# Float64 words to float32 in five steps with an integer add, and raw quarters of w_out loaded into the place of W

## The chip, the cores and the metric

The kernel runs on one core of a Trainium2 chip. The metric is the device time of one execution in microseconds (us). Its engines are TensorE (PE in the profile, with PEld for its weight loads), VectorE (DVE), ScalarE (ACT), GpSimd (POOL) and SyncE (SP), which here only issues transfers.

## The reference

Three parts follow each other, in float32, save that two of the weights reach the chip as raw float64:

```python
k_p = k.reshape(B, H, Sp, 8, D).mean(axis=3)          # keys and values pooled by 8
attn = softmax(q @ k_p.T / sqrt(D)); x = attn @ v_p    # 8 heads, 4608 tokens, 512 wide
logits = x @ phi                                       # 8 experts x 4 slots
slot_input = softmax(logits, axis=0).T @ x
slot_out[e] = maximum(slot_input[e] @ w1[e], 0) @ w2[e]
x = softmax(logits, axis=1) @ slot_out
h = x @ w_in                                           # w_in, w_out: float64 on arrival
solu = h * softmax(h)
ln = (solu - mean) / sqrt(var + 1e-6) * g_ln
out = ln @ w_out
```

## The kernel before

There are three stages. In the attention stage the tokens go in 12 blocks of 384; a scheduler of the language orders the instructions of PE, DVE, ACT and POOL there, from a list of due times. In the experts' stage 32 slot rows pass through eight experts: `first(e)` (L674) multiplies by w1, `second(e, fh)` (L835) by w2, half an expert at a time, for `x` from 0 to 15. Between the halves other work is written out by hand or fitted in by the scheduler: the combine weights are copied (`combine_copies`, L792, tile c), turned (L799, pc) and split (L801 on ACT, L802 on DVE, tile cS), and the two float64 weights are converted. In the last stage, from the first h (L949) on, 36 tiles of 128 tokens go through the h product, the softmax, the layer norm and the product with w_out (L1108 to L1111), in an order written by hand.

w_in and w_out arrive in four raw quarters each, 128 x 2048 words of 4 bytes (1 MB): o0 to o3 for w_out, i0 to i3 for w_in. The two words of a float64 lie side by side. A conversion makes a float32: ACT takes the absolute value of the high word, scaled (L715), DVE shifts it by three bits (L735), puts the sign in (L736), makes a power of two of the exponent (L737), multiplies it with the low word (L745), and POOL adds the two in float (L731). The quarters of w_in go to four tiles win0 to win3, which the product pM (L889) reads after the last `second`. Those of w_out go to yo; ACT squares them for a sum over all (L755, into W_lo as scratch), and `out_scale` (L760 to L766: the product pq, a power on POOL, the scales gs) waits for all four. Then come W_hi (L769, eight on ACT) and W_lo (L772, eight on DVE): here called the W stage, at x == 9.

SP issues transfers in the order written: `SEQ` names them, o and i for raw quarters, b for the w2 of an expert (two of 1 MB), a for w1, W for the tiles win (no transfer). Raw quarters take one of two buffers of `rawp`, w1, w2 and win a ring of 88 KB a partition. A transfer whose buffer isn't free waits at the head of SP's queue, and all behind it wait too. `CI` says ahead of which x a quarter is converted, `DUM` after which x a product without use is put that keeps PE busy (L861, spare).

Of the kernel before, what the change touches and what calls it, by code (L numbers as in the profile page):

```python
# [19 lines left out]
P = 128  # L20
# [8 lines left out]
DM = 512  # L29
# [16 lines left out]
PST = 0  # L46
LP = ()
LS = 2
OL = 0
# [3 lines left out]
for e_, m_ in AP: BESIDE[e_] += m_  # L53
WQ = 2
WQ2 = 4
SEQ = 'o0 a1 a2 r4 b0 b1 a5 a6 o1 i0 b3 i1 b2 o2 b5 W0 o3 b6 i2 b4 i3 b7'.split()
WL = 0
NPRE = 8
OA = ((1,), (1,), (1,), (1,), (1,), (1,), (1,), (1,), (1,), (1,), (1,), (1,))
# [24 lines left out]
def moe_attention_kernel(ctx: ExitStack, tc, q, k, v, phi, w1, w2, w_in, w_out, g, out):  # L84
    nc = tc.nc
    pe, dve, act, pool, sp = nc.tensor, nc.vector, nc.scalar, nc.gpsimd, nc.sync
# [9 lines left out]
    g_sb = cpool.tile([P, NFC], F32, name="g_sb")  # L96
# [66 lines left out]
    w1t, wo_raw, w2t, wi_raw, win = {}, {}, {}, {}, {}  # L163
# [7 lines left out]
                store[e, (i + j) // 4, (i + j) % 4] = t[:, j, :]  # L171

    def load_raw(store, src, i, name):
        store[i] = (ring if OL and i == 1 and store is wo_raw else rawp).tile([P, 2048], I32, name="raw")
        sp.dma_start(store[i], src[i].bitcast(I32))

    placed = {}
# [43 lines left out]
    if True:  # L221
# [476 lines left out]
    if True:  # L698
        ex = ctx.enter_context(tc.tile_pool(name="ex", bufs=1, side="left", reuse_waits="tile"))
        cvp = ctx.enter_context(tc.tile_pool(name="cvp", bufs=2, side="left", reuse_waits="tile"))  # L700
# [3 lines left out]
        pool.memset(hTm, 0.0)  # L704


        mag, last_s = {}, [None]

        def words(raw):
            w = raw.rearrange("p (n two) -> p n two", two=2)  # L710
            return w[:, :, 0], w[:, :, 1]

        def double_size(key, raw, pl=None):
            y = mag[key] = cvp.tile([P, 1024], F32, name="cv_y") if pl is None else pl.bitcast(F32)
            act.activation(y, words(raw)[1].bitcast(F32), AF.Abs, scale=2.0 ** -112)  # L715

        def double_steps(key, dst, raw, pl=None):
            lo, hi = words(raw)
            yf = mag[key]
            y = yf.bitcast(I32)  # L720
            s = cvp.tile([P, 1024], I32, name="cv_s") if pl is None else pl.bitcast(I32)
            sf = last_s[0] = s.bitcast(F32)

            def low():

                act.activation(lo.bitcast(F32), lo.bitcast(U32), AF.Copy, scale=2.0 ** -52)

            last = (
                (lambda: pool.scalar_tensor_tensor(sf, lo.bitcast(U32), 2.0 ** -52, sf, ALU.mult, ALU.mult)) if PST else
                (lambda: pool.tensor_tensor(sf, lo.bitcast(F32), sf, ALU.mult)),  # L730
                lambda: pool.tensor_tensor(dst, yf, sf, ALU.add),  # L731
            )

            return low, (
                lambda: dve.tensor_scalar(y, y, 3, None, ALU.logical_shift_left),  # L735
                lambda: dve.scalar_tensor_tensor(y, hi, -(1 << 31), y, ALU.bitwise_and, ALU.bitwise_or),  # L736
                lambda: dve.tensor_scalar(s, y, -(1 << 23), None, ALU.bitwise_and),  # L737
            ), last

        def from_double(key, dst, raw):  # L740
            low, steps, last = double_steps(key, dst, raw)
            for f in steps:
                f()
            if True:
                dve.scalar_tensor_tensor(last_s[0], words(raw)[0].bitcast(U32), 2.0 ** -52, last_s[0], ALU.mult, ALU.mult)  # L745
            last[1]()


        yo = ex.tile([P, NFC, DM], F32, name="yo")

        def out_words(i):
            y = yo[:, 2 * i:2 * i + 2, :].rearrange("p c d -> p (c d)")
            from_double(("o", i), y, wo_raw[i])
            for c in (2 * i, 2 * i + 1):
                act.activation(W_lo[:, c, :].bitcast(mybir.dt.bfloat16), yo[:, c, :], AF.Square, scale=g_sb[:, c:c + 1], accum_out=wsq[:, c:c + 1])  # L755

        def out_scale():

            pq = psE.tile([P, NFC], F32, name="pq", tag="spare")
            pe.matmul(pq, ones, wsq, start=True, stop=True)  # L760
            dve.tensor_reduce(ws[:, 0:1], pq, axis=AX.X, op=ALU.add)
            dve.tensor_scalar(ws[:, 0:1], ws[:, 0:1], 1e-30, 2.0 ** -30, ALU.max, ALU.mult)
            pool.tensor_tensor(ws[:, 1:2], ws[:, 0:1], exps_[:, 0:1], ALU.pow)
            dve.tensor_scalar(ws[:, 1:2].bitcast(I32), ws[:, 1:2].bitcast(I32), 0x7F800000, None, ALU.bitwise_and)
            dve.reciprocal(ws[:, 2:3], ws[:, 1:2])
            dve.tensor_scalar(gs, g_sb, ws[:, 1:2], None, ALU.mult)  # L766

        def high_part(c):
# [26 lines left out]
        def combine_split(i):  # L795
            c4 = c4s.pop(i)
            pc = psE.tile([P, 4, P], F32, name="pc", bufs=2)
            for t in range(4):
                pe.transpose(pc[:, t, :], c4[:, t].rearrange("p a s -> p (a s)"), ident)  # L799
            cd = cS[:, 4 * i:4 * i + 4, :]  # L800
            act.activation(cd, pc, AF.Copy)  # L801
            dve.scalar_tensor_tensor(cd, cd.bitcast(F32), lo_rows, pc, ALU.mult, ALU.add)  # L802

        for x in SEQ[NPRE:]:
            load_next(x)

        double_size(("o", 0), wo_raw[0])
        double_size(("o", 1), wo_raw[1])
        out_words(0)
        out_words(1)  # L810
        combine_exps()
# [26 lines left out]
        for i in range(2):  # L838
            combine_copies(i)
        CE = (0, 0, 0, 2, 9, 13, 14, 14, 15)  # L840
        CI = {0: (("i", 0),), 2: (("i", 1),), 4: (("o", 2),), 6: (("o", 3),), 8: (("i", 2),), 10: (("i", 3),)}
        for x in range(2 * NE):
            for kind, i in CI.get(x, ()):
                double_size((kind, i), (wi_raw if kind == "i" else wo_raw)[i])
                if kind == "i":
                    from_double(("i", i), win[i], wi_raw[i])
                else:
                    out_words(i)
            if x == 9:
                out_scale()  # L850
                for c in range(NFC):
                    high_part(c)
                    low_part(c)
            for i in range(9):
                if CE[i] == x:
                    combine_split(i)
                    if i + 2 < 9:
                        combine_copies(i + 2)
            second(x // 2, x % 2)
            for nn in DUM.get(x, ()):  # L860
                pe.matmul(spare[:, 0:nn], ident, w2t[x // 2, x % 2, 3][:, 0:nn], start=True, stop=True)  # L861
# [38 lines left out]
        for hf in range(2):  # L900
# [327 lines left out]
```

## Time and profile before

| | |
|---|---|
| time, median of 3 runs | 461.35 us (459.4 to 462.12) |
| time of the profiled execution | 462.56 us |
| span from its first to its last instruction | 460.7 us |
[...]
| PE, DVE, ACT, POOL busy | 408.5, 340.7, 287.8, 225.3 us |
| transfers | 97.06 MB |

The 1.86 us between span and time lie outside the instructions. Times in the profile count from the span's start. The shares of busy time are averages over stages with different limits, so the experts' stage is read from timelines of its own.

### The profile page before, as it was taken

The numbers are of one execution on the slowest core, as the hardware profiler recorded it, in microseconds if no ns is written. First come the engines' busy times: TensorE is split into PE (matmuls) and PEld (weight loads), VectorE is DVE, ScalarE is ACT, GpSimd is POOL, SyncE is SP. The second block draws the span as 40 slices with busy tenths as digits, with TensorE's granted clock in tenths as the row PEclk, the third lists the DMA queues.
The fourth block names the chain that finished last, engine by engine and source line by source line (L and its number), as shares of the span: only waits on it lengthen the run. The fifth ranks groups of instructions, "written<-read, shape, count | busy, mean of one in ns | idle before, by whom it ended". The sixth has DMA issues, their size and how long they took to land. (4 is left out here: it accounts for less than half of the span.)

```text
span 460.7 us, 8267 instructions
## 1 busy us (share of the span) xinstructions
PE 408.5 (89%) x2979; PEld 229.6 (50%) x2979; DVE 340.7 (74%) x563; ACT 287.8 (62%) x645; POOL 225.3 (49%) x392
## 2 busy tenths in 40 slices
PE   4688998998999797833967999999999999999997
PEld 4376576786777424222313544444444444444445
DVE  4798498999893557785929988777878888778710
ACT  4476675995785406333624995777877886878721
POOL 4485176665341017693221566665555555565510
PEclk9778999999999787965979999999999999999999
DMA  8999986692598788999200034858659666675851
GB/s 287 421 416 419 418 324 268 195 336 101 199 370 276 234 317 368 345 379 366 95 1 0 0 94 91 167 102 188 156 104 177 160 161 114 159 159 94 161 149 56
DMA packets 84008, 97.06 MB, mean 211 GB/s; under 512 B 70017, under 2 KB 70785, under 8 KB 78849
## 3 DMA queue, kind: packets, MB, share of 16 engines
q1 hardware_dynamic: 83968, 96.55, 66.6%
q8 instruction: 23, 0.38, 0.3%
q14 instruction: 17, 0.13, 0.1%
HBM read 70.32 MB, written 9.44 MB: 173 GB/s over the span
## 5 line engine op out<-in xcount | busy, mean ns | idle before, releaser
L1108 PE MATMUL o<-W_hi,vhi 128*128 128x512 f16 x280 | 106.4, 380 | 0.7 <-ACT vhi L1017 0.6
L1109 PE MATMUL o<-W_lo,vhi 128*128 128x512 f16 x280 | 106.1, 379 | 0.0
L339 PE MATMUL sc<-BD,qT 128*128 128x144 f32 (+1 forms) x320 | 59.9, 334 | 12.0 <-ACT BD L282 7.9
L1111 PE MATMUL o<-W_hi,vlo 128*128 128x512 f16 x280 | 67.3, 379 | 0.6 <-DVE vlo L997 0.6
L377 POOL TENSOR_TENSOR a<-a,rs 128x864 f32<-128x864 f32 x23 | 37.5, 1641 | 57.0 <-DVE rs L375 45.3
L339 PEld LDWEIGHTS sc<-BD,qT 128*128 128x128 f32 (+1 forms) x320 | 45.0, 203 | 23.3 <-issue 7.8
L1088 ACT ACTIVATE v<-u,b,sr 128x1024 f32<-128x1024 f32 x33 | 40.9, 1240 | 15.1 <-POOL b L1087 15.0
L1098 DVE TENSOR_TENSOR v<-v,v 128x1024 f16<-128x1024 f32 x32 | 39.2, 1224 | 10.8 <-ACT v L1088 10.8
L1108 PEld LDWEIGHTS <-vhi 128*128 128x128 f16 x280 | 27.3, 98 | 38.6 <-issue 7.5
L1065 ACT ACTIVATE e<-u,nmu 128x1024 f32<-128x1024 f32 x33 | 37.9, 1148 | 13.5 <-POOL nmu L1064 12.8
L1060 ACT ACTIVATE e<-h,nm 128x1024 f32<-128x1024 f32 x33 | 36.7, 1111 | 13.4 <-DVE nm L1057 13.2
L1111 PEld LDWEIGHTS <-vlo 128*128 128x128 f16 x280 | 27.2, 98 | 33.5 <-DVE vlo L997 1.0
L1057 DVE TENSOR_REDUCE nm<-h 128x1 f32<-128x1024 f32 x33 | 40.1, 1220 | 3.8 <-PE h L1054 3.7
L1062 DVE CUSTOM_DVE_ANT_0 u<-h,e 128x1024 f32<-128x1024 f32 x33 | 40.3, 1221 | 3.4 <-ACT e L1060 3.0
L1109 PEld LDWEIGHTS <-vhi 128*128 128x128 f16 x280 | 27.4, 98 | 30.1 <-issue 0.9
L1097 DVE TENSOR_SCALAR v<-u,nmu,sr 128x1024 f16<-128x1024 f32 x32 | 26.0, 812 | 18.7 <-POOL sr L1074 18.6
L349 DVE TENSOR_REDUCE nmax<-sc 128x6 f32<-128x432 f32 x48 | 28.5, 600 | 10.8 <-PE sc L339 10.5
L384 PE MATMUL pt<-ident,a 128*128 128x128 f32 (+1 forms) x180 | 31.8, 285 | 1.3 <-ACT aT L391 0.8
L391 ACT ACTIVATE aT<-pt 128x384 f32<-128x384 f32 (+1 forms) x60 | 27.7, 486 | 7.2 <-PE pt L384 6.7
L1077 POOL TENSOR_SCALAR r<-sr,ws 128x1 f32<-128x1 f32 x33 | 29.1, 881 | 3.4
L1074 POOL TENSOR_TENSOR sr<-z,exponents 128x3 f32<-128x3 f32 x33 | 28.9, 877 | 2.7
L1124 ACT ACTIVATE ob<-o,r 128x512 f32<-128x512 f32 x32 | 21.4, 669 | 9.6 <-PE o L1111 9.6
(224 smaller groups left out, 773.4 us busy)
## 6 DMA issues: line engine op xcount, KB each, us to landing
w<-in_w_dram SPq DMA_DIRECT2D x16, 1024.0 KB, 9.6
vT<-in_v_dram SPq DMA_DIRECT2D x8, 1152.0 KB, 12.7
qT<-in_q_dram SPq DMA_DIRECT2D x11, 768.0 KB, 17.6
out_dram<-ob SPq DMA_DIRECT2D x11, 768.0 KB, 3.7
w<-in_w_dram SPq DMA_DIRECT2D x16, 512.0 KB, 6.9
kT<-in_k_dram SPq DMA_DIRECT2D x7, 1152.0 KB, 18.7
raw<-in_w_out_dram SPq DMA_DIRECT2D x4, 1024.0 KB, 14.1
raw<-in_w_in_dram SPq DMA_DIRECT2D x4, 1024.0 KB, 8.1
```

Of the source, the lines that this page charges most:

```text
L339: pe.matmul(sc[t0:t1, r].rearrange("p h j -> p (h j)"), qT[n][:, hp, r, t0:t1], BD[b % NBD][:, hp, :], start=True, stop=True)
L377: eng.tensor_tensor(av, av, rs.unsqueeze(3).to_broadcast([P, NR, 4, J]), ALU.mult)
L384: pe.transpose(pt[:m, r, :], a_buf[n % NA][:, r, P * c:P * c + m], ident)
L1057: dve.tensor_reduce(nm, hv, axis=AX.X, op=ALU.max, negate=True)
L1060: act.activation(e, hv, AF.Exp, bias=nm, accum_out=st[:, 0:1])
L1062: dve.tensor_tensor_reduce(u, hv, e, 1.0, 0.0, ALU.mult, ALU.add, st[:, 1:2])
L1065: act.activation(e, u, AF.Square, bias=nmu, accum_out=st[:, 2:3])
L1088: act.activation(v, u, AF.Identity, bias=b, scale=sr[:, 0:1])
L1098: eng[H2].tensor_tensor(v2, v, v1, ALU.subtract)
L1108: pe.matmul(po, hi[:, c, :], W_hi[:, c, :], start=(c == 0), stop=False)
L1109: pe.matmul(po, hi[:, c, :], W_lo[:, c, :], start=False, stop=False)
L1111: pe.matmul(po, lo[:, c, :], W_hi[:, c, :], start=False, stop=(c == NFC - 1))
```

## The change

The conversion has five steps: ACT takes the high word as before (L720 of the new kernel) and turns the low word, in place, into an integer scaled by 2 to the -29 (L721); DVE shifts and puts the sign in (L722, L723); POOL adds the two as 32-bit integers (L724). The steps L737 and L745 on DVE are gone. o2 and o3 are loaded into the memory of W_hi and W_lo instead of the buffers of `rawp`, the squares go to a scratch tile of their own (cv_q), and the W stage stands ahead of x == 4 instead of 9. `SEQ` and `CI` have a new order.

```diff
-SEQ = 'o0 a1 a2 r4 b0 b1 a5 a6 o1 i0 b3 i1 b2 o2 b5 W0 o3 b6 i2 b4 i3 b7'.split()
+SEQ = 'o0 a1 a2 r4 b0 b1 a5 a6 o1 b2 o2 o3 b3 i0 W0 b4 i1 b5 i2 b6 i3 b7'.split()
     def load_raw(store, src, i, name):
-        store[i] = (ring if OL and i == 1 and store is wo_raw else rawp).tile([P, 2048], I32, name="raw")
+        if store is wo_raw and i > 1:
+            store[i] = (W_hi, W_lo)[i - 2].rearrange("p c d -> p (c d)").bitcast(I32)
+        else:
+            store[i] = rawp.tile([P, 2048], I32, name="raw")
         sp.dma_start(store[i], src[i].bitcast(I32))
-        def double_size(key, raw, pl=None):
-            y = mag[key] = cvp.tile([P, 1024], F32, name="cv_y") if pl is None else pl.bitcast(F32)
-            act.activation(y, words(raw)[1].bitcast(F32), AF.Abs, scale=2.0 ** -112)
...
-                lambda: pool.tensor_tensor(dst, yf, sf, ALU.add),
...
-                lambda: dve.tensor_scalar(y, y, 3, None, ALU.logical_shift_left),
-                lambda: dve.scalar_tensor_tensor(y, hi, -(1 << 31), y, ALU.bitwise_and, ALU.bitwise_or),
-                lambda: dve.tensor_scalar(s, y, -(1 << 23), None, ALU.bitwise_and),
...
-                dve.scalar_tensor_tensor(last_s[0], words(raw)[0].bitcast(U32), 2.0 ** -52, last_s[0], ALU.mult, ALU.mult)
+        def from_double(dst, raw, add):
             lo, hi = words(raw)
+            y = cvp.tile([P, 1024], F32, name="cv_y")
+            yi = y.bitcast(I32)
+            act.activation(y, hi.bitcast(F32), AF.Abs, scale=2.0 ** -112)
+            act.activation(lo, lo.bitcast(U32), AF.Copy, scale=2.0 ** -29)
+            dve.tensor_scalar(yi, yi, 3, None, ALU.logical_shift_left)
+            dve.scalar_tensor_tensor(yi, hi, -(1 << 31), yi, ALU.bitwise_and, ALU.bitwise_or)
+            add.tensor_tensor(dst.bitcast(I32), yi, lo, ALU.add)
...
-        CI = {0: (("i", 0),), 2: (("i", 1),), 4: (("o", 2),), 6: (("o", 3),), 8: (("i", 2),), 10: (("i", 3),)}
+        CI = {3: (("o", 2),), 4: (("o", 3),), 7: (("i", 0),), 9: (("i", 1),), 11: (("i", 2),), 13: (("i", 3),)}
...
-            if x == 9:
+            if x == 4:
                 out_scale()
                 for c in range(NFC):
                     high_part(c)
```

On SP, in the experts' stage, the queue behind the last of expert 6's w1 stood so before (raw is a quarter, from in_w_in or in_w_out; w2_70 and w2_74 are the halves of b7):

```order
L175 DMA raw_2302<-in_w_out_dram 128x2048
L169 DMA w2_50_2304<-in_w2_dram 128x2048
L169 DMA w2_54_2306<-in_w2_dram 128x2048
L175 DMA raw_2312<-in_w_out_dram 128x2048
L169 DMA w2_60_2314<-in_w2_dram 128x2048
L169 DMA w2_64_2316<-in_w2_dram 128x2048
L175 DMA raw_2318<-in_w_in_dram 128x2048
L169 DMA w2_40_2320<-in_w2_dram 128x2048
L169 DMA w2_44_2322<-in_w2_dram 128x2048
L175 DMA raw_2324<-in_w_in_dram 128x2048
L169 DMA w2_70_2326<-in_w2_dram 128x2048
L169 DMA w2_74_2328<-in_w2_dram 128x2048
```

And so it stands in the changed kernel, its last twelve, behind b2, o2, o3 (into W_hi and W_lo) and b3:

```order
L179 DMA raw_2300<-in_w_in_dram 128x2048
L169 DMA w2_40_2306<-in_w2_dram 128x2048
L169 DMA w2_44_2308<-in_w2_dram 128x2048
L179 DMA raw_2310<-in_w_in_dram 128x2048
L169 DMA w2_50_2312<-in_w2_dram 128x2048
L169 DMA w2_54_2314<-in_w2_dram 128x2048
L179 DMA raw_2316<-in_w_in_dram 128x2048
L169 DMA w2_60_2318<-in_w2_dram 128x2048
L169 DMA w2_64_2320<-in_w2_dram 128x2048
L179 DMA raw_2322<-in_w_in_dram 128x2048
L169 DMA w2_70_2324<-in_w2_dram 128x2048
L169 DMA w2_74_2326<-in_w2_dram 128x2048
```

All of w_out now comes ahead of w_in; i0 to i3 (raw_2300 to raw_2322) share the two buffers of `rawp` with o0 and o1 alone, and i3 with b7 behind it is last as before.

On POOL, the adds of the conversions stand among the copies c of the combine weights. Before, from the copy behind the add of i0 on:

```order
L792 TENSOR_TENSOR c_2415<-L_all,cr 128x512
L731 TENSOR_TENSOR win_2309<-cv_y,cv_s 128x1024
L792 TENSOR_TENSOR c_2424<-L_all,cr 128x512
L792 TENSOR_TENSOR c_2449<-L_all,cr 128x512
L792 TENSOR_TENSOR c_2538<-L_all,cr 128x512
L731 TENSOR_TENSOR yo<-cv_y,cv_s 128x1024
L792 TENSOR_TENSOR c_2573<-L_all,cr 128x512
L792 TENSOR_TENSOR c_2588<-L_all,cr 128x512
L731 TENSOR_TENSOR yo<-cv_y,cv_s 128x1024
L763 TENSOR_TENSOR ws<-ws,exponents 128x1
L731 TENSOR_TENSOR win_2310<-cv_y,cv_s 128x1024
L731 TENSOR_TENSOR win_2311<-cv_y,cv_s 128x1024
```

Now, from the second copy behind the add of o2 on (W_lo holds the raw words of o3):

```order
L771 TENSOR_TENSOR c_2405<-L_all,cr 128x512
L724 TENSOR_TENSOR yo<-cv_y,W_lo 128x1024
L771 TENSOR_TENSOR c_2414<-L_all,cr 128x512
L771 TENSOR_TENSOR c_2431<-L_all,cr 128x512
L771 TENSOR_TENSOR c_2524<-L_all,cr 128x512
L742 TENSOR_TENSOR ws<-ws,exponents 128x1
L771 TENSOR_TENSOR c_2563<-L_all,cr 128x512
L724 TENSOR_TENSOR win_2302<-cv_y,raw 128x1024
L771 TENSOR_TENSOR c_2578<-L_all,cr 128x512
L724 TENSOR_TENSOR win_2303<-cv_y,raw 128x1024
L724 TENSOR_TENSOR win_2304<-cv_y,raw 128x1024
L724 TENSOR_TENSOR win_2305<-cv_y,raw 128x1024
```

The adds of w_out and the power ws moved ahead of all four adds of w_in.

On ACT, the low words of o0 and o1 are converted in the attention stage, in its fifth block of 12. Before, from the end of the fourth block's transposes on:

```order
L281 ACTIVATE BD_206<-kp 64x2x72
L282 ACTIVATE BD_206<-kp 64x2x72
L315 ACTIVATE WT<-pw_809 32x144 x4
L355 ACTIVATE a_225,ssum<-sc_761,nmax 128x72 x6
L361 ACTIVATE a_225<-dd_207 128x3x144
L324 ACTIVATE W<-pW_823 128x128
L325 ACTIVATE W<-pW_823 64x32
L361 ACTIVATE a_225<-dd_208 128x3x144
```

Now:

```order
L285 ACTIVATE BD_206<-kp 64x2x72
L286 ACTIVATE BD_206<-kp 64x2x72
L721 ACTIVATE raw<-raw 128x1024
L319 ACTIVATE WT<-pw_809 32x144 x4
L359 ACTIVATE a_225,ssum<-sc_761,nmax 128x72 x6
L365 ACTIVATE a_225<-dd_207 128x3x144
L328 ACTIVATE W<-pW_823 128x128
L329 ACTIVATE W<-pW_823 64x32
L721 ACTIVATE raw<-raw 128x1024
L365 ACTIVATE a_225<-dd_208 128x3x144
```

Two instructions came in. Behind this place the scheduler has put many of the attention stage's instructions in another order on PE, DVE and ACT, none of them new.

## Rows read from the trace of the kernel before

**Rows 1.** Page: PE's busy tenths in 40 slices of the span.

```profile
PE   4688998998999797833967999999999999999997
```

**Rows 2.** Timeline of PE, 215 to 242 us: start, length, instructions, idle time before.

```profile
215.69 0.59 PE L760 MATMUL pq<-wsq,ones 128*128 128x8 f32 x2 [7.06 <-ACT W_lo L755]
...
220.21 6.22 PE L835 MATMUL p<-w,hTm 128*32 128x512 f32 x56
...
226.98 1.07 PE L835 MATMUL p<-w,hTm 128*32 128x512 f32 x8
...
230.27 1.06 PE L889 MATMUL pM<-win,so 128*32 128x512 f32 x6 [0.37 <-ACT so L882]
235.01 3.62 PE L889 MATMUL pM<-win,so 128*32 128x512 f32 x10 [3.68 <-POOL win L731]
238.56 2.76 PE L1001 MATMUL pM<-hTm,sel 128*128 128x512 f32 x4
241.87 0.51 PE L949 MATMUL h<-MS,cS 128*128 128x512 f32 x1 [0.56 <-DVE MS L1008]
```

**Rows 3.** Timeline of DVE, 215 to 242 us.

```profile
221.18 7.51 DVE L772 SCALAR_TENSOR_TENSOR W_lo<-yo,gs,W_hi 128x512 f16<-128x512 f32 x8
228.61 0.68 DVE L735 TENSOR_SCALAR cv_y<-cv_y 128x1024 int32<-128x1024 int32 x1
229.32 1.23 DVE L736 SCALAR_TENSOR_TENSOR cv_y<-raw,cv_y 128x1024 int32<-128x1024 int32 x1
```

**Rows 4.** Timeline of POOL, 187 to 236 us.

```profile
189.36 3.37 POOL L731 TENSOR_TENSOR win<-cv_y,cv_s 128x1024 f32<-128x1024 f32 x1
...
216.75 1.10 POOL L763 TENSOR_TENSOR ws<-ws,exponents 128x1 f32<-128x1 f32 x1 [2.67 <-DVE ws L762]
...
232.62 2.34 POOL L731 TENSOR_TENSOR win<-cv_y,cv_s 128x1024 f32<-128x1024 f32 x1 [8.46 <-DVE cv_s L745]
```

**Rows 5.** Timeline of SP's queue, 160 to 215 us: issues of transfers.

```profile
173.57 11.14 SPq L169 DMA_DIRECT2D w<-in_w_dram  x2
...
211.66 0.33 SPq L175 DMA_DIRECT2D raw<-in_w_in_dram  x1
212.09 0.84 SPq L169 DMA_DIRECT2D w<-in_w_dram  x2
```

**Rows 6.** Busy time by stretch: engines (us, instructions), PE's clock, DMA share, GB/s.

```profile
195.00:200.00 5.00, 0.64 (x3) 0.67 (x4) 4.97 (x5) 0.07 (x1) 4.46 (x3) 0.92 1.02 429
...
210.00:215.00 5.00, 0.00 (x0) 0.00 (x0) 1.59 (x2) 0.89 (x3) 2.41 (x1) 0.50 0.86 334
...
220.00:225.00 5.00, 5.00 (x50) 1.50 (x52) 4.97 (x4) 5.00 (x9) 2.83 (x1) 1.00 0.28 118
```

**Rows 7.** Groups, shapes apart, 176 to 242 us: busy us, mean ns, idle before.

```profile
L792 POOL TENSOR_TENSOR c<-L_all,cr 128x512 f32<-128x512 f32 x9 | 12.2, 1367 | 8.5 <-PE pc L799 7.5 <-ACT h L819 1.1
L731 POOL TENSOR_TENSOR win<-cv_y,cv_s 128x1024 f32<-128x1024 f32 x4 | 10.9, 2721 | 11.9 <-DVE cv_s L745 11.9
L736 DVE SCALAR_TENSOR_TENSOR cv_y<-raw,cv_y 128x1024 int32<-128x1024 int32 x6 | 8.8, 1463 | 0.1
...
L745 DVE SCALAR_TENSOR_TENSOR cv_s<-raw,cv_s 128x1024 f32<-128x1024 uint32 x6 | 8.1, 1342 | 0.1
...
L735 DVE TENSOR_SCALAR cv_y<-cv_y 128x1024 int32<-128x1024 int32 x6 | 6.8, 1138 | 4.4 <-ACT cv_y L715 4.4
L715 ACT ACTIVATE cv_y<-raw 128x1024 f32<-128x1024 f32 x6 | 6.8, 1137 | 2.4 <-POOL win L731 2.4
L802 DVE SCALAR_TENSOR_TENSOR cS<-cS,lo_rows,pc 128x512 fp32r<-128x512 f32 x9 | 6.4, 739 | 1.4 <-ACT cS L801 1.4
...
L737 DVE TENSOR_SCALAR cv_s<-cv_y 128x1024 int32<-128x1024 int32 x6 | 4.1, 688 | 0.1
```

**Rows 8.** Timeline of ACT, 168 to 262 us: first square of o1.

```profile
182.15 0.71 ACT L755 ACTIVATE W_lo<-yo,g_sb 128x512 bf16<-128x512 f32 x1
```

**Rows 9.** Busy time by stretch in the attention stage, columns as in rows 6.

```profile
40.00:50.00 10.00, 8.07 (x59) 4.93 (x58) 5.69 (x8) 6.24 (x24) 3.61 (x4) 0.83 1.00 412
```

More of the change, by code (lines that the diff above doesn't have):

```diff
@@ L704, in moe_attention_kernel @@
         pool.memset(hTm, 0.0)
-        mag, last_s = {}, [None]
         def words(raw):
@@ L711, in words @@
             return w[:, :, 0], w[:, :, 1]
-        def double_size(key, raw, pl=None):
-            y = mag[key] = cvp.tile([P, 1024], F32, name="cv_y") if pl is None else pl.bitcast(F32)
-            act.activation(y, words(raw)[1].bitcast(F32), AF.Abs, scale=2.0 ** -112)
-        def double_steps(key, dst, raw, pl=None):
+        def from_double(dst, raw, add):
             lo, hi = words(raw)
[L719 to L730, printed above, removed]
-                lambda: pool.tensor_tensor(dst, yf, sf, ALU.add),
-            )
-            return low, (
-                lambda: dve.tensor_scalar(y, y, 3, None, ALU.logical_shift_left),
-                lambda: dve.scalar_tensor_tensor(y, hi, -(1 << 31), y, ALU.bitwise_and, ALU.bitwise_or),
-                lambda: dve.tensor_scalar(s, y, -(1 << 23), None, ALU.bitwise_and),
[L738 to L744, printed above, removed]
-                dve.scalar_tensor_tensor(last_s[0], words(raw)[0].bitcast(U32), 2.0 ** -52, last_s[0], ALU.mult, ALU.mult)
-            last[1]()
+            y = cvp.tile([P, 1024], F32, name="cv_y")
[5 more added lines that the diff above has]
+            add.tensor_tensor(dst.bitcast(I32), yi, lo, ALU.add)
         yo = ex.tile([P, NFC, DM], F32, name="yo")
@@ L752, in out_words @@
             y = yo[:, 2 * i:2 * i + 2, :].rearrange("p c d -> p (c d)")
-            from_double(("o", i), y, wo_raw[i])
+            from_double(y, wo_raw[i], pool)
             for c in (2 * i, 2 * i + 1):
-                act.activation(W_lo[:, c, :].bitcast(mybir.dt.bfloat16), yo[:, c, :], AF.Square, scale=g_sb[:, c:c + 1], accum_out=wsq[:, c:c + 1])
+                sq = cvp.tile([P, DM], mybir.dt.bfloat16, name="cv_q", bufs=1)
+                act.activation(sq, yo[:, c, :], AF.Square, scale=g_sb[:, c:c + 1], accum_out=wsq[:, c:c + 1])
         def out_scale():
@@ L805, in moe_attention_kernel @@
             load_next(x)
-        double_size(("o", 0), wo_raw[0])
-        double_size(("o", 1), wo_raw[1])
         out_words(0)
@@ L840, in moe_attention_kernel @@
         CE = (0, 0, 0, 2, 9, 13, 14, 14, 15)
-        CI = {0: (("i", 0),), 2: (("i", 1),), 4: (("o", 2),), 6: (("o", 3),), 8: (("i", 2),), 10: (("i", 3),)}
+        CI = {3: (("o", 2),), 4: (("o", 3),), 7: (("i", 0),), 9: (("i", 1),), 11: (("i", 2),), 13: (("i", 3),)}
         for x in range(2 * NE):
             for kind, i in CI.get(x, ()):
-                double_size((kind, i), (wi_raw if kind == "i" else wo_raw)[i])
                 if kind == "i":
-                    from_double(("i", i), win[i], wi_raw[i])
+                    from_double(win[i], wi_raw[i], pool)
                 else:
                     out_words(i)
-            if x == 9:
+            if x == 4:
                 out_scale()
```

## The prediction

> **What bounds the kernel now.** The page's strip of busy tenths comes first: from slice 21 on PE stands at 9 to the end [rows 1]. So the last stage, from the first h at 241.87 to the span's end at 460.7, is 218.8 us of PE that this change leaves alone. What the change can bring is an earlier first h.
>
> Ahead of it the timeline of PE has holes [rows 2]. It does nothing for 7.06 us ahead of pq, since the squares of o3 come late; then come the second half of the `second` products, to 228.05, and a hole of 3.68 us until win3 is ready at 235.0; h follows the end of pM (238.63) by 3.24. Why win3 is late stands on DVE: the eight W_lo end at 228.69, and only then come i3's four steps [rows 3], and POOL's add from 232.62 to 234.96 [rows 4]. The W stage in turn waited for pq, at 215.7.
>
> The second bound is the transfers. i3 is issued at 211.66 and b7 right behind it [rows 5]; the queue's share in 220 to 225 is 0.28 [rows 6], so it falls quiet at about 221.4, which is 9.7 us behind the issue of i3. Before, that is early enough: its last half is used at 226.98 [rows 2].
>
> **The change, part by part.** *The steps taken out.* DVE loses L737 and L745, for six quarters in this stage 4.1 + 8.1 = 12.2 us [rows 7]; ACT gains the low word, six at about the 1.14 of L715 [rows 7], 6.8 us. The low word runs on ACT while DVE does its two steps, so it costs nothing on the path, save where ACT is itself the next to be waited for. POOL adds as often as before.
>
> *The order.* i3's conversion no longer stands behind the W stage, which moves up to x == 4. But i3 and b7 are still last in SP's queue, and i3 takes the buffer of i1, which POOL's add of i1 gives back. That add comes late: in the order of DVE the steps of i1 stand behind all eight W_lo. So the sum is the path from the squares of o1 to the add of i1, then the transfers behind i3, then the end of the stage. What comes ahead of 182 us I take as unchanged.
>
> The bounds come from two sets of lengths. Short: the shift 0.68, the sign 1.23 [rows 3], the add 2.34 [rows 4], a copy c 1.17, half the add's price for half the elements. Long: the means 1.14, 1.46, 2.72 and 1.37 [rows 7], which hold what DVE and POOL cost each other. ACT's steps are 1.14 either way. No row has an integer add on POOL or an integer result on ACT: I take each as the float row of its engine that is nearest.
>
> From 182.85, when the first square of o1 is through [rows 8], short and long:
> - ACT's high word of o2 to 184.0; DVE's two steps to 185.9 or 186.6; POOL's add of o2 to 188.2 or 189.3.
> - Two copies c and the add of o3 on POOL, in its order: to 193.6 or 194.8. (The first copy needs the first pc, about 188.9.)
> - ACT's two squares of 0.7, then pq 0.59 [rows 2], to 196.0 or 197.4. POOL has three copies c to do ahead of the power ws, which is 1.10 [rows 4]: to 198.2 or 200.0.
> - DVE in its order: i0's two steps, two splits of 0.74 [rows 7], the small steps to gs: 200.2 or 202.3. W_lo begins one W_hi later (0.6 to 0.7, as long as a square [rows 8]) and takes 7.51 [rows 3]: 208.4 or 210.4.
> - Two more splits, 1.5; i1's two steps 1.9 or 2.6; the add of i1: 214.1 or 217.2. SP issues i3 at 214.2 or 217.3; the middle is 215.75, against 211.66 before [rows 5].
>
> b7 then lands by the 9.7 us of before: 225.45 in the middle. The transfers go quiet in between. The second half of b3 waits for the ring as the last of two issues of before did, to about 184.4 [rows 5]; with it ten transfers of 1 MB stand ahead of i3, at 429 GB/s [rows 6] 2.44 us each, so they are through by about 209. That gap of 5 to 8 us is the price of i3's buffer.
>
> From b7 to h the length depends on PE's clock. [...] At full speed: the last `second` 1.07, then 2.22 to the start of pM, pM at 6 records in 1.06, so 16 in 2.8, and 3.24 to h [rows 2]: 9.3. At half speed: 2.1, 3.3 (the second product ps doubled), pM at 10 records in 3.62, so 16 in 5.8, and 3.24: 14.4. I take the middle, 11.9, since the work becomes dense only with b7.
>
> Win3 is beside that path: i3 lands two transfers ahead of b7, at 220.6; the high word, DVE's two steps and the add give 227.0 at the long lengths, and pM begins at 228.7 at the soonest (225.45 + 1.07 + 2.22).
>
> **The sum.** h at 225.45 + 11.9 = 237.35 in place of 241.87: 4.5 us earlier. The bounds are 214.2 + 9.7 + 9.3 = 233.2 (8.7 earlier) and 217.3 + 9.7 + 14.4 = 241.4 (0.5 earlier). The profiled execution took 462.56, and would take 458.0; the median of before, 1.2 us below it, is 461.35, so I forecast 456.8.
>
> [...] POOL's add took 3.37 us once and 2.34 another time [rows 4]; the long one ran beside DVE's last step on i1. [...] I keep the middle, since the add of i1 has DVE quiet beside it.
>
> **The rivals.**
> 1. *The integer add is slow.* Three adds lie on the path in a row, so each us more costs three. From 4.0 us an add the gain is gone. At twice the mean, 5.4, the path is 8.7 longer: 465.5, slower. For it: no row has such an add. [...]
> 2. *The attention stage is put out.* ACT gets two steps of 1.14 in its fifth block, and from there the scheduler has reordered PE. PE is short of work for 1.9 us of 40 to 50 [rows 9], and ACT idles 3.8 there, so the two steps fit in; but an order that loses 5 us ahead of the first w1 product gives no change, 461.8, and one that loses 8 gives 464.8.
> 3. *The transfers hold it all.* If i1's add ends at 220 (ACT's work on i0, two cS and the W stage standing ahead of i1's high word), b7 lands at 229.8 and h comes at 241.7: 461.2, no change.
> 4. *The add is cheap, and SP's queue never stops.* At 1.2 us an add, three times 1.3 are saved: 452.8. The limit is the queue without a gap: thirteen transfers from 184.4 and the 2.4 that the 9.7 hold over three of them, b7 at 218.5, h at 230.4: 449.9. For it: nothing but that the price is unknown below as above. Against: no row shows a cheaper add of two tensors.
>
> **How the numbers follow.** Changes of up to 0.5%, 2.3 us, are what a measurement of this kernel can't tell from none. My forecast has 0.50, of which 0.46 gains more than that; rival 1 0.08; rival 2 0.17, of which 0.08 slower, 0.06 no change, 0.03 faster since a new order can also win; rival 3 0.12; rival 4 0.13. Faster: 0.46 + 0.03 + 0.13 = 0.62. The same: 0.04 + 0.06 + 0.12 = 0.22. Slower: 0.16. The range goes from 452.0, where rival 4 stands, to 461.8, past the no-change cases; what lies above is the slow sides of rivals 1 and 2, what lies below the limit of rival 4.
>
> **What will show it.** Right: pq near 196, W_lo over by 208 to 211, i3's issue at 214 to 217 behind POOL's add of i1, transfers idle some us ahead of it, PE waiting for b7 and not for win3, the first h at 233 to 241. An add on POOL well over 3 us shows rival 1; a first w1 product (L674) that starts 2 us or more away from where it does now shows rival 2; i3 issued ahead of 212 shows rival 4. What would prove me wrong is a conversion whose length none of these rows has, or a wait for win ahead of pM.

## The result, and the profile after

| | before | after |
|---|---|---|
| median | 460.77 us (4 runs, 459.40 to 462.12) | 455.44 us (4 runs, 454.25 to 457.47) |
| ratio | | 0.9889, 95% interval 0.9841 to 0.9937 |
| profiled execution, its span | 462.56, 460.7 | 455.15, 452.8 |
| its mean granted TensorE clock | 0.937 | 0.959 |
| first h to the end of the span | 218.8 | 218.6 |

The change is 1.1% faster; 456.8 was forecast. Run once more, 12 times beside 21 of before, it took 457.17 against 461.98: 0.9914 (0.9885 to 0.9944). The last stage keeps its length, so all of the gain is an earlier first h: 234.24 in place of 241.87.

TensorE's timeline of the changed kernel (start, length, instructions, idle time before and what ended it), answering [rows 2]:

```profile
195.43 0.39 PE L739 MATMUL pq<-wsq,ones 128*128 128x8 f32 x2
...
208.77 1.09 PE L778 MATMUL pc<-ident,c 128*128 128x128 f32 x4 [4.33 <-DVE cS L781]
...
221.07 1.94 PE L812 MATMUL p<-w,hTm 128*32 128x512 f32 x8 [5.82 <-DMA w<-in_w_dram]
222.94 1.22 PE L837 MATMUL spare<-w,ident 128*128 128x256 f32 x2
224.09 1.86 PE L812 MATMUL p<-w,hTm 128*32 128x512 f32 x8
226.74 1.08 PE L854 MATMUL ps<-sel,s 128*128 128x32 f32 x8 [0.79 <-ACT s L851]
228.19 2.73 PE L865 MATMUL pM<-win,so 128*32 128x512 f32 x16 [0.37 <-ACT so L858]
...
234.24 0.50 PE L925 MATMUL h<-MS,cS 128*128 128x512 f32 x1 [0.56 <-DVE MS L984]
```

The two waits of before are gone: pq comes 20 us earlier, and pM no longer waits for win3. In their place the longest is one of 5.82 us for b7, a transfer. SyncE's queue and POOL say why b7 is late ([rows 5, 4]):

```profile
201.78 0.33 SPq L179 DMA_DIRECT2D raw<-in_w_in_dram  x1
...
213.72 0.33 SPq L179 DMA_DIRECT2D raw<-in_w_in_dram  x1
214.15 0.85 SPq L169 DMA_DIRECT2D w<-in_w_dram  x2
```

```profile
191.27 2.41 POOL L724 TENSOR_TENSOR yo<-cv_y,W_lo 128x1024 int32<-128x1024 int32 x1
...
199.35 2.40 POOL L724 TENSOR_TENSOR win<-cv_y,raw 128x1024 int32<-128x1024 int32 x1
...
211.28 2.42 POOL L724 TENSOR_TENSOR win<-cv_y,raw 128x1024 int32<-128x1024 int32 x1 [8.53 <-DVE cv_y L723]
...
221.84 2.38 POOL L724 TENSOR_TENSOR win<-cv_y,raw 128x1024 int32<-128x1024 int32 x1 [3.82 <-DVE cv_y L723]
```

POOL's add of i1 ends at 213.70, and i3 is issued at 213.72, with b7 behind it. By stretch ([rows 6]: busy us and instructions of PE, its weight loads, DVE, ACT and POOL, then PE's clock, DMA share, GB/s):

```profile
205.00:210.00 5.00, 1.23 (x8) 0.92 (x12) 4.97 (x9) 4.97 (x8) 0.00 (x0) 0.87 1.01 418
210.00:215.00 5.00, 5.00 (x30) 1.59 (x22) 4.97 (x4) 2.60 (x3) 2.42 (x1) 0.79 0.33 105
...
220.00:225.00 5.00, 3.92 (x18) 0.91 (x18) 1.67 (x2) 0.74 (x1) 2.38 (x1) 0.50 0.56 234
```

The transfers are quiet for two thirds of 210 to 215, and go quiet for good at about 222.8 (0.56 of the next stretch). The two second products that use b7 then take 1.94 and 1.86 us at a granted clock of 0.50 and 0.55, where before the last took 1.07 at 1.00 [rows 2]. VectorE, answering [rows 3]:

```profile
186.20 2.23 DVE L722 TENSOR_SCALAR cv_y<-cv_y 128x1024 int32<-128x1024 int32 x1 [0.89 <-ACT cv_y L720]
...
199.86 1.93 DVE L745 TENSOR_SCALAR gs<-g_sb,ws 128x8 f32<-128x8 f32 x1
202.58 5.39 DVE L751 SCALAR_TENSOR_TENSOR W_lo<-yo,gs,W_hi 128x512 f16<-128x512 f32 x8 [0.79 <-ACT W_hi L748]
...
209.20 0.69 DVE L722 TENSOR_SCALAR cv_y<-cv_y 128x1024 int32<-128x1024 int32 x1
...
211.72 2.52 DVE L722 TENSOR_SCALAR cv_y<-cv_y 128x1024 int32<-128x1024 int32 x1
```

The eight W_lo take 5.39 in place of 7.51, but gs, 8 columns wide, takes 1.93.

**The stage ahead.** The prediction's second rival was an attention stage put out by the new low words. ScalarE's rows in it, of the change and then of before (its row of the four WT copies is the last that both have in one place):

```profile
48.97 1.13 ACT L721 ACTIVATE raw<-raw 128x1024 int32<-128x1024 uint32 x1
51.89 1.17 ACT L319 ACTIVATE WT<-pw 32x144 f32<-32x144 f32 x4 [1.79 <-PE pw L316]
...
55.56 1.18 ACT L721 ACTIVATE raw<-raw 128x1024 int32<-128x1024 uint32 x1
```

```profile
53.77 1.17 ACT L315 ACTIVATE WT<-pw 32x144 f32<-32x144 f32 x4 [2.94 <-PE pw L312]
```

The first w1 product starts at 160.37 in the change and at 159.30 before. That is 1.07 later, under the 2 us which the prediction set as the sign. But the WT copies had come 1.88 earlier, so from there the change took 108.48 where before took 105.53. What comes ahead of the WT copies varies from execution to execution (50.4 to 56.0 in the 14 profiles, and by 3.0 between e9 and e10 below, whose attention stage is the same), so the next table counts from landmarks.

All times in us, from one profile of each kernel: WT copies to the first w1 product; that product to pq, to i3's issue and to the first h. The medians are those of all runs; each ratio is to the runs of before made beside that kernel, whose medians were 460.77 to 462.21.

| kernel | WT to w1 | w1 to pq | to i3 | to h | median | ratio, interval |
|---|---|---|---|---|---|---|
| before | 105.53 | 56.39 | 52.36 | 82.57 | 460.77 | |
| change | 108.48 | 35.06 | 53.35 | 73.87 | 455.44 | 0.9889 (0.9841 to 0.9937) |
| c5, change again | 110.74 | 34.80 | 53.08 | 71.95 | 457.17 | 0.9914 (0.9885 to 0.9944) |
| e1, steps only | 108.37 | 53.44 | 51.87 | 75.19 | 459.59 | 0.9938 (0.9900 to 0.9975) |
| e2, order only | 104.49 | 42.28 | 55.02 | 77.67 | 458.18 | 0.9894 (0.9849 to 0.9939) |
| e3, i3's own room | | | 45.44 | | 454.15 | 0.9796 (0.9730 to 0.9862) |
| e4, busy wait | 110.66 | 34.94 | 53.22 | 74.47 | 458.09 | 0.9905 (0.9868 to 0.9941) |
| e6, o0 and o1 in seven | 107.23 | 34.58 | 52.86 | 71.72 | 455.64 | 0.9858 (0.9800 to 0.9916) |
| e7, gs on ScalarE | 109.43 | 36.74 | 54.80 | 74.88 | 457.20 | 0.9904 (0.9873 to 0.9934) |
| e8, e6 with e3 | | | 41.87 | | 451.62 | 0.9778 (0.9720 to 0.9835) |
| e9, low words late | 107.23 | 35.33 | 53.61 | 74.04 | 453.82 | 0.9834 (0.9794 to 0.9874) |
| e10, e9 with e3 | 104.50 | 36.99 | 44.69 | 74.10 | 450.48 | 0.9772 (0.9728 to 0.9816) |
| e11, i1's add twice | 108.40 | 37.68 | 58.74 | 78.67 | 461.73 | 0.9989 (0.9959 to 1.0019) |
| e12, i2's, i3's twice | 108.26 | 35.98 | 54.28 | 74.60 | 458.16 | 0.9936 (0.9902 to 0.9970) |

The profiles of e3 and e8 are of executions over 1.5% above the fastest of their kernels, so only the place of i3's issue is read from them. Where w1 to pq is above 36.5 in a kernel with the change's order and steps, ph, the products between those with w1 and those with w2, took 3.62 us in place of 1.97 (e7, e10 and e11), which adds about 1.7 to the columns behind it. In the change its 1.97 were at a granted clock of 1.00; in the profile of before ph took 3.40 at 0.54, so up to 1.4 of its 56.39 may be chance of the same kind.

### The profile page after: what moved, and what is told of

The parts are those of the page before. It is cut to its first block, busy times and chain, and to the rows that moved or that the text cites. A ratio compares the mean times of both kernels' runs of the same rounds, so it can differ in the third digit from the quotient of the medians.

```text
span 452.8 us, 8266 instructions
## 1 busy us (share of the span) xinstructions
PE 405.0 (89%) x2979; PEld 224.1 (49%) x2979; DVE 323.8 (72%) x547; ACT 296.0 (65%) x653; POOL 222.1 (49%) x392
## 5 line engine op out<-in xcount | busy, mean ns | idle before, releaser
L395 ACT ACTIVATE aT<-pt 128x384 f32<-128x384 f32 (+1 forms) x60 | 28.0, 488 | 11.8 <-PE pt L388 11.4
L812 PE MATMUL p<-w,hTm 128*32 128x512 f32 x128 | 21.1, 742 | 7.1 <-DMA w<-in_w_dram 6.5
```

## The experiments

**e1, the steps without the order.** The kernel before, with the change's from_double in place of its seven steps; SEQ, CI, the buffers and the place of the W stage stay.

```diff
-                lambda: dve.tensor_scalar(s, y, -(1 << 23), None, ALU.bitwise_and),
-                dve.scalar_tensor_tensor(last_s[0], words(raw)[0].bitcast(U32), 2.0 ** -52, last_s[0], ALU.mult, ALU.mult)
-                lambda: pool.tensor_tensor(dst, yf, sf, ALU.add),
+            act.activation(lo, lo.bitcast(U32), AF.Copy, scale=2.0 ** -29)
+            add.tensor_tensor(dst.bitcast(I32), yi, lo, ALU.add)
```

> The kernel before with the five-step conversion alone: its order of loads, its buffers and the place of the W stage stay. Theory A (the steps carry the gain: before, h waited for win3, which stood behind o3's squares, the W stage and i3's conversion on DVE): four quarters lose about 2 us each of DVE's work ahead of the squares of o3, so pq comes at 207 to 210 in place of 215.7, the W stage ends by about 222, win3 by about 227 and h at 231 to 236, for 452 to 456. Theory B (the new order carries it): pq stays within 2 us of 215.7 and the time is that of before, 459 to 462.

Neither theory held as a whole: the time, 459.59, is in B's range, 0.6% under before, but not for B's reason. From w1 to h the steps save 7.4 us (82.57 to 75.19). Of that 5.0 lie behind the start of the last second product (14.89 to 9.89), where the 3.68 that pM waited for win3 are gone; pq comes only 3.0 earlier where A had 6 to 9. And 2.8 us go again between the WT copies and w1 (108.37). POOL and the queue of e1 show why pq gained so little:

```profile
177.14 5.89 POOL L719 TENSOR_TENSOR yo<-cv_y,raw 128x1024 int32<-128x1024 int32 x2
...
200.99 2.40 POOL L719 TENSOR_TENSOR win<-cv_y,raw 128x1024 int32<-128x1024 int32 x1
```

```profile
179.59 0.33 SPq L175 DMA_DIRECT2D raw<-in_w_in_dram  x1
...
203.42 0.33 SPq L175 DMA_DIRECT2D raw<-in_w_out_dram  x1
```

And before, for the same two loads, i0 and o3:

```profile
165.11 0.37 SPq L175 DMA_DIRECT2D raw<-in_w_in_dram  x1
...
190.56 0.33 SPq L175 DMA_DIRECT2D raw<-in_w_out_dram  x1
```

The integer add reads the raw quarter itself, so the buffer is given back only when POOL is through (203.39 for i1's), and o3's load waits for it (203.42); in the seven steps VectorE's last pass gave it back (190.49). That is more than the length of one add, since POOL comes late to its adds: the load of i0, which waits for the add of o0, is issued 15.3 behind the first w1 product in place of 5.8, and o3's 39.1 behind it in place of 31.3. So in e1 the five steps hold the raw buffers longer. The change, with o2 and o3 in the place of W_hi and W_lo, does not need the buffers of o0 and o1 so early.

**e2, the order without the steps.** The changed kernel with the seven-step conversion.

```diff
-            act.activation(lo, lo.bitcast(U32), AF.Copy, scale=2.0 ** -29)
-            add.tensor_tensor(dst.bitcast(I32), yi, lo, ALU.add)
+            dve.tensor_scalar(s, y, -(1 << 23), None, ALU.bitwise_and)
+            dve.scalar_tensor_tensor(sf, lo.bitcast(U32), 2.0 ** -52, sf, ALU.mult, ALU.mult)
+            add.tensor_tensor(dst, yf, sf, ALU.add)
```

> The changed kernel with the old conversion (two more passes of DVE, no low word on ACT, a float add on POOL) in its place: the loads, buffers and the early W stage of the change stay. Theory A (each quarter costs DVE 2 us more on the path to i1's conversion, and i3's issue waits for DVE's last pass on i1): pq at 199 to 201, i3's issue at 217 to 221, h at 237 to 241, for 456.5 to 460. Theory B (the order carries the gain, the steps lie in the shade of the transfers): i3's issue within 2 us of 213.7 and 454.5 to 456.5.

From w1 to h it saves 4.9, and pq comes 7.2 to 7.5 later than in the two profiles of the change, as A had it. i3's issue comes only 1.7 to 1.9 later, as B had it: here the buffer is free at VectorE's last pass on i1, over at 213.45, without the add, and i3 is issued at 213.52. The time, 458.18, is in A's range. So both halves carry a part, 7.4 and 4.9, and together (8.7 and 10.6 in the two profiles of the change) less than their sum. These are single profiles with the clock in them: from the start of the last second product to h e2 took 12.19, e1 9.89. In the medians e2 alone is as fast as the whole change, which fits its attention stage without low words: 104.49 from WT to w1.

**e3, room for i3.** One raw quarter is loaded into the ring.

```diff
-            store[i] = rawp.tile([P, 2048], I32, name="raw")
+            store[i] = (ring if store is wi_raw and i == 3 else rawp).tile([P, 2048], I32, name="raw")
```

> The changed kernel with i3's raw quarter loaded into the ring of the expert pieces in place of i1's buffer, so that its load waits for a second product that is done by about 202 and no longer for POOL's add of i1. My theory (the stop of the queue behind i1's add sets when b7 lands): i3 is issued at about 203, the queue does not fall quiet between 205 and 215, b7 lands at 218 to 220 in place of 222.8, h comes 3 to 5 us earlier, 450.5 to 453. Rival (the transfers hold b7 by their bytes anyway, or another wait follows right behind): h less than 1 us earlier, 454.5 to 456.

i3 is issued 45.44 behind the first w1 product in place of 53.35, right behind b6; 0.9796 against 0.9889 and 0.9914; its interval lies below c5's and overlaps that of the first comparison. The stop of the queue was worth about 1%, as my theory had it, though the median, 454.15, fell between my range and the rival's.

**e4, TensorE busy in the wait.**

```diff
-        DUM = {10: (512,), 14: (256,), 11: (128,), 13: (256, 256)}
+        DUM = {10: (512,), 14: (256,), 11: (128,), 13: (256, 256) + (512,) * 4}
```

> The changed kernel with four more products of 128x512 into the spare bank behind those of x == 13, in the 5.8 us in which TensorE waits for b7 (their result is not read). My theory (TensorE idles there, and 0.50 of its clock is granted when b7 comes): the two last second products take about 1.07 us each in place of 1.94 and 1.86, and h comes 1.5 to 2.5 us earlier, 453 to 454. Rival (the clock does not follow TensorE's own idle time, or s and ps hold it): granted clock in 220 to 225 stays near 0.50 and the time stays within 0.7 us of 455.4.

```profile
216.08 4.56 PE L837 MATMUL spare<-w,ident 128*128 128x256 f32 x12
223.05 1.06 PE L812 MATMUL p<-w,hTm 128*32 128x512 f32 x8 [2.41 <-DMA w<-in_w_dram]
...
225.52 1.94 PE L812 MATMUL p<-w,hTm 128*32 128x512 f32 x8 [0.56 <-DMA w<-in_w_dram]
228.23 1.92 PE L854 MATMUL ps<-sel,s 128*128 128x32 f32 x8 [0.78 <-ACT s L851]
```

The first product on b7 is fast now (1.06), but the next and ps take 1.94 and 1.92 (in the change ps took 1.08 at 1.00). The granted clock was 0.94 in 220 to 225 and 0.50 in 225 to 230. What was idle still is, 2.41 us ahead of the first, and the 0.50 came one product later. The tail from the last second product to h is 11.36 against 10.15 and 8.56, and the time is the change's, not the 453 to 454 of my theory. In this profile the filling moved the slow stretch and did not remove it.

**c5, e6, e9, the attention stage.** c5 is the change itself. e6 keeps seven steps for o0 and o1 alone; e9 keeps five everywhere and ties each low word behind its high word:

```diff
-            act.activation(y, hi.bitcast(F32), AF.Abs, scale=2.0 ** -112)
-            act.activation(lo, lo.bitcast(U32), AF.Copy, scale=2.0 ** -29)
+            high = act.activation(y, hi.bitcast(F32), AF.Abs, scale=2.0 ** -112)
+            after(act.activation(lo, lo.bitcast(U32), AF.Copy, scale=2.0 ** -29), high)
```

> The changed kernel itself, beside the next three on one chip. My theory of the attention stage: in the four profiles with the five-step conversion of o0 and o1 the way from ScalarE's four WT copies of the fifth block to the first w1 product took 108.4 to 110.7 us, in the two with the seven steps 104.5 and 105.5, so this profile shows 108 to 111 again, and 455 to 457. Rival (those differences are chance of the clock): 104 to 107 here.

> The changed kernel with the seven-step conversion kept for o0 and o1 alone, which lie in the attention stage; o2, o3 and w_in take five steps. TensorE's order of the attention stage is then that of before, with no low word on ScalarE in it. My theory (the two low words made the scheduler reorder the attention stage, which costs 3 to 5 us): from the WT copies to the first w1 product 104 to 106 us, from that product to the first h 73 to 75 as in the change, 2.5 to 4.5 us under the change run beside it, so about 452. Rival (the attention stage is the same length either way): within 1 us of the change.

> The changed kernel with one line more: each low word on ScalarE stands behind its own high word, so that those of o0 and o1 no longer run in the middle of the attention stage (at 49.0 and 55.6 in the change) but behind it, and TensorE's order of that stage is that of before. All quarters keep five steps. My theory (the order of the attention stage, not the number of steps, costs): from the WT copies to the first w1 product 104.5 to 107.3 us against 108.5 and 110.7 in the two profiles of the change, 1.5 to 4 us faster than the change, 453 to 455.5. Rival (the low words cost by themselves or the difference was chance): 108 to 111, and 456.5 to 458.

In e9 the low words of o0 and o1 stand behind the attention stage:

```profile
53.45 1.16 ACT L319 ACTIVATE WT<-pw 32x144 f32<-32x144 f32 x4 [2.95 <-PE pw L316]
...
159.45 1.12 ACT L720 ACTIVATE cv_y<-raw 128x1024 f32<-128x1024 f32 x1 [0.60 <-PE pT L510]
160.48 1.19 ACT L721 ACTIVATE raw<-raw 128x1024 int32<-128x1024 uint32 x1
```

L720 waits there for cv_y, whose room is the attention stage's until then, and in e9 the low word waits for L720; in the change the low word, which writes in place, had nothing to hold it back, and was put at 49.0. From WT to w1, e6 and e9 took 107.23, e2 and e10 104.5, before 105.5; the seven profiles used that have the low words in the stage (the change, c5, e1, e4, e7, e11, e12) 108.3 to 110.7. (e8, left out of those columns above, has the order of before and took 109.98; 0.57 of the clock was granted there in the stretch named below.) e9's interval lies below c5's (0.9874 and 0.9885 are their near ends), though it overlaps that of the first comparison; its median is 3.4 under c5's, as forecast. e6 missed: 107.23 in place of 104 to 106, and a median only 1.5 under c5's where 2.5 to 4.5 was forecast, with intervals that overlap. By the ratios of the four pairs (c5 to e6 and e9, e3 to e8 and e10) the low words in the attention stage cost 0.8 to 3.7 us; all point the same way, and the size is open. Part of the difference between the profiles is the clock: 60 to 70 us behind the WT copies 0.83 or 0.67 was granted in every one of those kernels, 1.00 in before, e2 and e10, and 0.83 in e6 and e9. What that is worth shows between e9 and e10, whose attention stage is the same: 107.23 and 104.50. So the lengths of single profiles do not separate the order from the clock.

**e7, gs on ScalarE.**

```diff
-            dve.tensor_scalar(gs, g_sb, ws[:, 1:2], None, ALU.mult)
+            act.activation(gs, g_sb, AF.Copy, scale=ws[:, 1:2])
```

> The changed kernel with one instruction moved: the 8-column product gs on ScalarE, which waits for it anyway, in place of VectorE. In the profile of the change it took 1.93 us on VectorE beside POOL's add of i0 and ended with that add; before it took 0.21. My theory (VectorE's instruction is held until POOL's add is through): gs takes under 0.4 us on ScalarE, W_hi begins about 1.5 us earlier, i3 is issued 1 to 2 us earlier against the first w1 product (52.0 in place of 53.35), and h comes 1 to 2 us earlier. Rival (it waits for something else, the power or the reciprocal): W_hi begins as before.

```profile
201.27 0.30 ACT L745 ACTIVATE gs<-g_sb,ws 128x8 f32<-128x8 f32 x1
```

```profile
202.54 2.45 DVE L751 SCALAR_TENSOR_TENSOR W_lo<-yo,gs,W_hi 128x512 f16<-128x512 f32 x1
```

gs takes 0.30, and W_hi begins 3.5 behind pq in place of 6.4. But the first W_lo now starts beside POOL's add of i0 (202.04 to 204.45) and takes 2.45 in place of about 0.7, and the eight end 12.3 us behind pq where they ended 12.5 behind it. i3 is issued 18.06 behind pq in place of 18.29, and the time is the change's: the 1 to 2 us that I forecast did not come. The wait was POOL's add, as I said; it passed to VectorE's next long instruction.

**e11 and e12, the adds.** The same add made twice, for i1, and for i2 and i3.

```diff
+            for _ in range(2 if again else 1):
-            add.tensor_tensor(dst.bitcast(I32), yi, lo, ALU.add)
+                add.tensor_tensor(dst.bitcast(I32), yi, lo, ALU.add)
```

> The changed kernel with POOL's add of i1 made twice, to the same place; the order of every engine is otherwise that of the change. My theory (i3's issue waits for the end of this add, b7 for i3, and h for b7): i3 is issued 2.4 us later against pq (20.7 in place of 18.3), b7 and h come 2.4 us later. Rival (b7 or h is held by something else, so the add has slack): h within 0.8 us of the change.

> The changed kernel with POOL's adds of i2 and i3 made twice; the order is otherwise that of the change. My theory (win2 and win3 are ready before b7's products and ps are through): win3 is ready 2.4 us later, at most at the start of pM, and from the last second products to h it takes what it took, 8.6 to 10.2 us. Rival (pM waits for win3, as in the kernel before): pM's first row names POOL's win as the releaser, and h comes 1 to 2.4 us later.

```profile
215.67 5.21 POOL L725 TENSOR_TENSOR win<-cv_y,raw 128x1024 int32<-128x1024 int32 x2 [8.52 <-ACT cS L781]
```

```profile
224.41 4.85 POOL L725 TENSOR_TENSOR win<-cv_y,raw 128x1024 int32<-128x1024 int32 x2 [1.94 <-DVE cv_y L723]
```

e11 puts i3's issue 21.06 behind pq in place of 18.29, 2.8 later, and h 40.99 in place of 38.81 and 37.15; its median is 4.6 above c5's, and its interval lies above those of the change. The add was forecast to cost 2.4; where the rest of the 4.6 comes from is not settled (in its one profile ph took 3.62 in place of 1.97). e12 has 2.4 more on each of two adds, no wait for win ahead of pM, 9.95 from the last second product to h, and a ratio whose interval overlaps the change's. The add of i1 is on the path, those of i2 and i3 are not.

**e8 and e10, both costs taken away.** e8 joins e6 and e3, e10 joins e9 and e3.

> The seven steps for o0 and o1 and i3's raw quarter in the ring, together. My theory (two separate costs: the attention stage, and the stop of the queue behind i1's add): the attention stage as in before, i3 issued about 45 us behind the first w1 product in place of 53, h 69 to 72 us behind it, and 5 to 8 us under the change run beside it, 448 to 451. Rival (the clock, which was at 0.50 between b7 and h in the run with i3's own room, gives the gain back): 451.5 to 454.

> The low words behind the attention stage, and i3's raw quarter in the ring. My theory: both gains add, i3 is issued 42 to 46 us behind the first w1 product, h 68 to 71 us behind it, 448.5 to 452, the fastest of these kernels. Rival (the second gain is given back to a lower clock between b7 and h): 452 to 455.

```profile
199.61 0.60 SPq L179 DMA_DIRECT2D raw<-in_w_in_dram  x1
```

```profile
205.00:210.00 5.00, 3.88 (x30) 1.19 (x30) 4.97 (x6) 3.94 (x5) 2.26 (x1) 1.00 1.02 428
210.00:215.00 5.00, 2.14 (x14) 0.88 (x12) 4.09 (x3) 2.15 (x2) 2.55 (x2) 0.86 0.96 397
215.00:220.00 5.00, 4.22 (x19) 0.84 (x11) 1.28 (x2) 0.66 (x2) 2.40 (x1) 0.50 0.02 7
```

e8's median, 451.62, is 5.6 under c5's, as forecast, but just past the 451 of my range and in the rival's. e10 is the fastest: 450.48, 0.9772 (0.9728 to 0.9816), 2.3% under before and over 1% under the change, whose intervals lie above it. Its transfers run without a gap to 215. The rival is seen in it as well: behind the wait for b7 0.50 was granted in 215 to 225 and 0.77 in 225 to 230, where h is (229.02); the way from the last second product to h took 11.86, so h stands 74.1 behind w1 where 68 to 71 was forecast, no nearer than in the change; against the 8.56 of c5 some 3 us of the gain went there. So this profile doesn't show the gain of i3's room in h. The median still fell, from 453.82 in e9 to 450.48; the intervals of the two overlap at 0.98, but all three pairs with and without i3's own room point the same way.

## Why the prediction came out right, point by point

The number was right, and so was the path behind it; but two terms were off in opposite directions, so that the forecast came within 1.4 us of the median is partly luck.

- *The path (squares of o1 to the add of i1).* Confirmed, at the short lengths or just under them: pq over at 195.82 (196.0 to 197.4 forecast), gs through at 201.79 (200.2 to 202.3), W_lo at 207.97 (208.4 to 210.4), the add of i1 at 213.70 (214.1 to 217.2), i3's issue at 213.72. e11 shows the tie of add, issue and h.
- *The lengths.* The term W_lo, 7.51 from [rows 3], was mis-sized: 5.39, with POOL idle beside all but the first of the eight. In before an add of 2.83 began 0.15 behind them (221.33), and in e7, where an add ran beside the first, the eight took 7.88. Against that gs took 1.93 where I had counted a small step.
- *The gap as the price of i3's buffer.* The gap is there, some 3 us in place of the forecast 5 to 8, since the transfers were through at about 211 and not at 209, and i1's add came at the short end. e3, e8 and e10 take it away and are faster by 0.6 to 1.2% than the change, e6 and e9.
- *b7 to h.* The whole was near, the parts were mis-sized. From the end of the transfers to h it took 11.4 in the change (222.8 to 234.24) and 9.9 in c5, where 11.9 was forecast. Left out of the sum was the time from that end to the start of the last second product, about 1.3, which waits for the first one and a spare product, at a granted clock of 0.50 (222.8 to 224.1). Too long were the terms behind it: from that start to h it was 10.15 and 8.56. Of the rows of before that stood for full speed the 3.24 ran at 0.77 (238.63 to 241.87), and the 2.8 was scaled up from six records in 1.06: in c5, where ps took 1.08 as it did at 1.00 in the change, pM takes 1.92 and h follows its end by 2.48. Half speed came into the sum from before, where 0.50 was granted in 210 to 215 with no TensorE work [rows 6]; that the middle of the two speeds would hold was my estimate.

```profile
226.05 1.94 PE L812 MATMUL p<-w,hTm 128*32 128x512 f32 x8
...
230.21 1.92 PE L865 MATMUL pM<-win,so 128*32 128x512 f32 x16 [0.37 <-ACT so L858]
232.07 1.98 PE L977 MATMUL pM<-hTm,sel 128*128 128x512 f32 x4
```

In the change 1.00 was granted from 226 to 229 and 0.50 again from 230 to 232, in the middle of pM (2.73); in e10, at 0.50 (220 to 225), pM took 3.64 where the bound at half speed had 5.8.
- *Win3 beside the path.* Confirmed: the add ended at 224.22, pM began at 228.19, and e12 could double it.
- *Rival 1, a slow integer add.* Falls: 2.37 to 2.43 for each of the six behind 182 us, the price of the float add with nothing beside it, 2.34 [rows 4].
- *Rivals 3 and 4.* i1's add ended at 213.70 and not at 220, and the queue did stop; e10 is rival 4's queue without a gap, and its median is near the 449.9 that the prediction gave as that limit, though its h stands 74.1 behind the first w1 product and the limit's 71.1.
- *3.37 or 2.34 for an add.* The long one of before [rows 4] did not come back on the path: its adds took 2.41 to 2.43, though VectorE's shift ran beside that of o2, and beside that of i1 too, where I had VectorE quiet (211.72 to 214.24). Here VectorE paid, 2.23 and 2.52 for the shift in place of 0.69 to 0.72; the 3.37 was an add that VectorE's pass had come before (last section).
- *Rival 2, the attention stage put out.* It came true in part, where I gave it 0.17: e9 puts it at 3.4 us of median beside c5, e6 at 1.5. The step that failed is "what comes ahead of 182 us I take as unchanged". My sign for it, the start of the first w1 product, missed it, since the start of the execution varies by as much.
- *The sum.* h was forecast at 237.35, 4.5 earlier, and came at 234.24: i3's issue 2.0 sooner than the middle, the transfers' end 9.1 behind it in place of 9.7, and 11.4 in place of 11.9. Behind the first w1 product the change gains 8.7 to 10.6, ahead of it it loses 3 to 5, and the medians show 5.3 and 4.8. The two errors nearly cancel.
- *A misreading.* On the strip of [rows 1] the 9s begin with slice 23; slices 21 and 22, with the first h in 22, show 6 and 7. No term of the sum hangs on it.

## What to carry to other kernels

Follow who gives a buffer back: here i3's load waited for the last reader of i1's raw quarter (the add's end 213.70, the issue 213.72) and held up b7 behind it (214.15), and in e1 the shorter conversion, whose last step reads the raw data, put o3's load 39.1 behind the first w1 product in place of 31.3. An in-place step without a buffer to wait for was moved far ahead by the scheduler (to 49.0, where e9 has it at 160.48), into a stage that by the ratios paid 0.8 to 3.7 us for it; one ordering edge took that back in the medians (453.82 in e9, 457.17 in c5). Where executions start differently (the WT copies came at 50.4 to 56.0), compare stages from a landmark that both kernels share, not from the start.

## What was not expected of the hardware

Some of VectorE's instructions took longer beside an add on POOL. With no add beside it the shift of 128x1024 took 0.69 to 0.72, and gs 0.21 in before; begun beside an add of the change they took 2.23 and 2.52, and 1.93, and each ended 0.04 to 0.56 us behind the add, which is no more than its own length (gs 201.79, the add 201.75). In e7 it was the first W_lo, 2.45 long and through at 204.99 where the add ended at 204.45. POOL's add had started first each time, kept its 2.4 (2.40 to 2.43), and it was VectorE's instruction that took longer. In before it was once the other way round: VectorE's L745 had begun at 188.54, and the add that began at 189.36 took 3.37 [rows 4] and ended 2.2 behind it.

Not every instruction of VectorE took longer, and what decides it no run shows. Beside the add of i0 (199.35 to 201.75) the reciprocal just ahead of gs took its 0.15, and the split of cS, which reads one tile beside TensorE's product pc, ran on beside the add of o3 (191.27 to 193.68) at its usual 0.7 each:

```profile
192.57 1.41 DVE L781 SCALAR_TENSOR_TENSOR cS<-cS,lo_rows,pc 128x512 fp32r<-128x512 f32 x2 [0.85 <-ACT cS L780]
...
199.79 0.15 DVE L744 RECIPROCAL ws<-ws 128x1 f32<-128x1 f32 x1
```

TensorE's granted clock was 0.50 in or soon behind its waits for b7: in the change 0.89 in 215 to 220 and 0.50 in 220 to 225 (a wait of 5.82 us), in e10 0.86 in 210 to 215 and 0.50 in 215 to 225 (2.86), in e4 0.94 in 220 to 225 and 0.50 in 225 to 230 (2.41, one product later). Products behind them take 1.9 in place of 1.07. What sets the granted clock, no run shows. The way from the last second product to h took 8.56 us in c5 and 11.86 in e10, whose instructions there are the same; the difference is more than half of what the whole change brings.
